# A new order list for attention and two feed-forward layers: the narrow token tile last, shared banks, interleaved pooled scores

## The chip, the cores and the metric

The kernel runs on one core of a Trainium2 chip. A core has five engines that work from instruction streams of their own: TensorE (PE in the profile, with its weight loads as PEld), VectorE (DVE), ScalarE (ACT), GpSimd (POOL) and SyncE (SP), which here only starts transfers. Sixteen DMA engines move data between HBM and the on-chip memory. Each engine takes its instructions strictly in program order, and waits at one until what it needs is there. The metric is the device time of one execution in microseconds, given as the median of several runs.

## What is computed

Attention over 4 batches, 8 heads and 576 positions, in two parts that are added: a pooled one (means over groups of 4 positions, so 144 by 144 scores, the result repeated 4 times) and a local one (only positions less than 4 apart). Its result is read as 2304 tokens of 512 values and goes through two feed-forward layers.

```python
def attention(q, k, v):                       # (4, 8, 576, 64)
    q_d, k_d, v_d = means over groups of 4    # (4, 8, 144, 64)
    out = repeat(softmax(q_d @ k_d.T / 8) @ v_d, 4)
    s = where(abs(i - j) < 4, q @ k.T / 8, -1e9)
    return out + softmax(s) @ v
x = attention(q, k, v) as (2304, 512)
h = x @ w_in                                  # 512 -> 2048
x2 = maximum(h, 0) ** 2 @ w_out               # 2048 -> 512
y = ((x2 @ w_a) * (x2 @ w_b)) @ w_out2        # 512 -> 1536 -> 512
```

## The kernel before

**Order.** The program is one hand-made list, `ORDER`, of tokens such as `H.0.3` or `ps.1.2.0.7`. A token calls one function, which writes its instructions; the order of the tokens is the order on every engine, and a letter (A, V, G, S) or a number in a token says which engine or which PSUM bank is used. So a token that stands earlier in the list puts its instructions ahead of all later ones on its engine, ready or not.

**First layer and attention.** Tokens are handled in units of 256, nine of them. `TILES` groups them to tiles: units 0-1, 2, 3-4, 5-6 and 7-8, that is 512, 256, 512, 512 and 512 tokens. For tile t, `H.t.f` computes block f of 16 of the hidden layer (12 matmuls, L648), `J` (three ScalarE steps, L655 to L658) and `L` (VectorE, L663) square it and split it into a high and a low part, and `P.t.f` (12 matmuls, L683) adds it to the four banks of x2. A matmul row in the profile is of 512 columns (a wide tile) or 256. The attention of units 0 to 4 (tokens b..) is done by TensorE in blocks with a band mask; that of units 5 to 8 (tokens l..) by VectorE and GpSimd, with products of 1792 columns (L416, L456) and sums (L424). The pooled attention (tokens p.., one per batch) computes scores in `scores` (L282): for each of 4 column groups ct of a batch and each of 2 heads, one call with two matmuls that use 64 of the 128 rows of the array, into one bank. Then come minima (L295), exponentials, transposes (L336) and values (L350). Attention of the units of one tile has to be complete before its `H`, and stands in the list between the blocks of the tile before.

**Warm-up.** `Z.k.n.bank` (L876) writes n transposes of the identity that nobody reads. There are 14 of them, 84 transposes, all ahead of `H.0.0`.

**Between the layers.** `E` copies a bank of x2 to the on-chip tile x2sb, `D` stores it in HBM (x2_d), and the second layer loads it from there. Of the last tile, only unit 7 goes this way; unit 8 stays on chip as xr2, split by `rh` (ScalarE) and `rl` (VectorE). `Q` frees the attention's buffers. `F.g.n` is step n of group g of what the second layer needs first: load and decode w_a and w_b (groups 0, 3, 4, 5) and load and split x2 of the first 1024 tokens, m = 0 (groups 1, 2, 6, 7). A split is a copy on ScalarE (L745, xb<-x2s), then a subtraction on VectorE (L742, xb<-x2s,xb).

**Second layer.** After the list, pool `ps` is closed and a pool of eight banks, `ps2`, is opened. The layer works in half sized blocks by a scheme with seven products: `hidden_span` computes for each j and m seven products for a and for b (12 wide matmuls in pairs, L916), and combines them in the banks and in the tiles r (r1 first: a ScalarE copy at L1012, which frees the bank for the next product). `hidden_rest` treats the unit left over from xr2 (48 narrow matmuls). Loads and splits for later steps, among them the second part m = 1 of x2, hang at numbered slots between the products (`put`).

Of the kernel before, what the change touches and what calls it, by code (L numbers as in the profile page):

```python
# [43 lines left out]
be.1.1 bc.1.0.0.V pj.0.0.2.V bm.0.1.0 bm.0.0.0 bx.0.0 bd.1.1 Z.11.6.7 pj.0.0.3.V pj.0.1.1.G sg be.0.0 pj.0.1.2.V
pq.0.A pj.0.1.3.V ps.0.2.0.4 ps.0.3.0.2 wd.1.S wd.8.S wc.1.A bd.0.0 wd.5.S ps.0.0.0.0 bq.0.1.S px.0.2.0 pe.0.2.0
wc.8.A bn.1.1.V wa.1 ps.0.0.1.4 wc.10.A ps.0.2.1.5 px.0.0.0 bn.0.0.V px.0.0.1 wa.8 bt.1.1.1.7 pe.0.0.1 pe.0.0.0 wh.8.G
px.0.2.1 px.0.3.0 pa.0.1.2 wd.0.S bc.1.1.1.V wa.10 wc.5.V pe.0.2.1 bt.0.0.0.6 wc.0.A wh.10.V Z.12.6.0 ps.0.1.0.1
wl.8.V pd.0.0 pd.0.2 wl.10.V bs.0.1.1.3 ps.0.3.1.0 bt.0.1.0.4 px.0.3.1 wa.5 bc.0.0.0.A pn.0.0.V pt.0.0.1.7 wh.1.A
# [87 lines left out]
def pooled_local_attention_two_ffn(  # L136
# [774 lines left out]
    def bank2():  # L911
        return ps2.tile([P, 512], F32, tag="b", name="bank")
# [408 lines left out]
```

## Time and profile before

| | before |
|---|---|
| median of 3 runs | 948.69 us (948.48 to 949.24) |
| the profiled execution | 950.97 us, of which the span is 949.2 us |
| mean granted clock of TensorE | 0.973 |
| busy: PE, DVE, ACT, POOL | 906.6, 568.2, 448.3, 302.5 us |
| first block of the first layer (`H.0.0`) starts | 65.8 us |
| last block of the first layer ends, second layer starts | 528 us |

The span is the time from the first to the last instruction on the core; 1.8 us of the execution lie around it. TensorE is busy nearly all the time, so the places to read are those where it is idle or where its granted clock is below 1. A timeline row gives the start, the time and the number of records of a run of like matmuls, and in brackets the idle time before it with the instruction that ended it.

### The profile page before, as it was taken

To read this page: it belongs to the slowest core of one execution; us is meant where nothing else is said; L and a number is where in the kernel's file an instruction comes from. 1 tells how busy PE (TensorE), PEld (TensorE's weight loads), DVE (VectorE), ACT (ScalarE), POOL (GpSimd) and SP (SyncE) were. 2 spreads that over 40 slices of the span, in tenths; PEclk is the share of its full clock that TensorE was granted. 3 is DMA by queue.
4 is the path that set the end of the run, shared out by engine and by line. 5 is a ranking of instruction groups with operands and counts; after the bars stand their busy time and mean duration, and the time that the engine had idled before them with its cause. 6 is when DMAs were issued, how large, how long until landed. Compare 5 with 4: busy or idle time off the path is not lost.

```text
span 949.2 us, 14089 instructions
## 1 busy us (share of the span) xinstructions
PE 906.6 (96%) x5084; PEld 755.9 (80%) x5084; DVE 568.2 (60%) x877; ACT 448.3 (47%) x1091; POOL 302.5 (32%) x286
## 2 busy tenths in 40 slices
PE   4799999999999999999999788999999999999998
PEld 3688877998877778887888576888888888788888
DVE  2768645442768768783114588686765654655451
ACT  3556456564534453334345445554454442554531
POOL 2232331211214541474011445565455450001010
PEclk9699999997999999999999798999999999999999
DMA  9575772641454204312300243875655649999522
GB/s 291 158 210 198 192 194 71 146 119 46 109 121 110 85 15 128 88 43 92 130 1 0 82 174 117 293 258 196 239 212 195 235 176 339 401 408 347 233 100 79
DMA packets 65854, 157.35 MB, mean 166 GB/s; under 512 B 7740, under 2 KB 11964, under 8 KB 65784
## 3 DMA queue, kind: packets, MB, share of 16 engines
q1 hardware_dynamic: 63336, 147.60, 45.2%
q0 software_dynamic: 2448, 8.85, 5.5%
q8 instruction: 40, 0.66, 0.3%
q14 instruction: 30, 0.25, 0.1%
HBM read 111.33 MB, written 45.09 MB: 165 GB/s over the span
## 4 chain that ended last, share of the span: by engine, by line
PE 90%; DVE 4%; ACT 1%; issue 1%; DVEq 0%
PE bank L916 40%; PE bank L648 21%; PE bank L683 21%; PE bank L282 2%; DVE xb L742 2%; PE bank L591 1%; PE bank L350 1%; PE bank L876 1%; PE bank L336 1%; PE bank L528 1%; PE bank L579 1%; DVE x2s L742 1%; DVE r L742 0%; PE bank L474 0%; DVE xx L496 0%
## 5 line engine op out<-in xcount | busy, mean ns | idle before, releaser
L916 PE MATMUL bank<-xb,wb 128*128 128x512 f32 x1008 | 236.6, 396 | 13.4 <-DVE xb L742 7.2
L916 PEld LDWEIGHTS bank<-xb,wb 128*128 128x128 f32 x1008 | 192.3, 192 | 55.7 <-DVE xb L742 9.0
L648 PE MATMUL bank<-xx,w 128*128 128x512 f32 (+1 forms) x960 | 214.8, 375 | 1.7 <-ACT xx L490 1.4
L683 PE MATMUL bank<-g,w 128*128 128x512 f32 (+1 forms) x960 | 212.3, 373 | 0.0
L648 PEld LDWEIGHTS bank<-xx,w 128*128 128x128 f32 x960 | 167.5, 190 | 36.9 <-ACT xx L490 3.3
L683 PEld LDWEIGHTS bank<-g,w 128*128 128x128 f32 x960 | 167.8, 190 | 32.9 <-issue 2.1
L916 PE MATMUL bank<-op,wo 128*128 128x512 f32 (+1 forms) x648 | 132.1, 366 | 1.6 <-DVE op L742 1.6
L916 PEld LDWEIGHTS bank<-op,wo 128*128 128x128 f32 x648 | 111.9, 189 | 21.9 <-DVE op L742 2.3
L663 DVE TENSOR_TENSOR g<-bank,g 128x512 fp32r<-128x512 f32 (+1 forms) x80 | 50.7, 634 | 119.1 <-ACT g L658 75.5
L742 POOL TENSOR_TENSOR wb<-raw,wb 128x256 fp32r<-128x256 f32 x96 | 80.8, 864 | 94.1 <-ACT wb L821 89.3
L655 ACT ACTIVATE bank<-bank 128x512 f32<-128x512 f32 (+1 forms) x80 | 43.3, 542 | 126.6 <-PE bank L648 126.6
L1012 ACT ACTIVATE r<-bank 128x512 f32<-128x512 f32 x72 | 42.8, 596 | 86.9 <-PE bank L916 80.3
L742 DVE TENSOR_TENSOR op<-ys,op 128x512 fp32r<-128x512 f32 x84 | 54.0, 707 | 31.3 <-ACT op L745 31.3
L966 DVE TENSOR_TENSOR r<-bank,r 128x512 f32<-128x512 f32 x48 | 32.9, 687 | 56.0 <-PE bank L916 41.7
L466 POOL TENSOR_TENSOR pv<-pv 128x768 f32<-128x768 f32 x16 | 34.9, 2181 | 84.2 <-DVE pv L456 84.2
L745 ACT ACTIVATE op<-ys 128x512 fp32r<-128x512 f32 x84 | 47.1, 624 | 25.1 <-PE bank L916 16.5
L222 DVE SCALAR_TENSOR_TENSOR raw<-raw,signs 128x512 uint32<-128x512 uint32 x68 | 49.0, 731 | 15.5 <-ACT signs L182 14.4
L658 ACT ACTIVATE g<-bank 128x512 fp32r<-128x512 f32 (+1 forms) x80 | 44.4, 555 | 20.9 <-PE bank L683 19.3
L742 POOL TENSOR_TENSOR wos<-raw,wos 128x256 fp32r<-128x256 f32 x48 | 43.1, 913 | 34.0 <-ACT wos L821 30.1
L821 ACT ACTIVATE wb<-raw 128x256 fp32r<-128x256 f32 x96 | 37.5, 425 | 16.4 <-DVE raw L222 8.8
L656 ACT ACTIVATE bank<-bank 128x512 f32<-128x512 f32 (+1 forms) x80 | 43.1, 539 | 2.5
L813 DVE TENSOR_TENSOR raw<-raw 128x256 f32<-128x256 f32 x72 | 41.9, 607 | 0.8
(121 smaller groups left out, 1021.9 us busy)
## 6 DMA issues: line engine op xcount, KB each, us to landing
ys<-y_d SPq DMA_DIRECT2D x42, 512.0 KB, 7.9
y_d<-r SPq DMA_DIRECT2D x72, 256.0 KB, 2.2
wo_d<-wos SPq DMA_DIRECT2D x48, 256.0 KB, 2.8
raw<-in_w_out SPq DMA_DIRECT2D x16, 511.8 KB, 3.9
raw<-in_w_in SPq DMA_DIRECT2D x16, 511.8 KB, 4.4
wo<-wo_d SPq DMA_DIRECT2D x24, 256.0 KB, 6.9
wo<-wo_d SPq DMA_DIRECT2D x12, 512.0 KB, 7.0
raw<-in_w_b SPq DMA_DIRECT2D x12, 511.8 KB, 4.1
```

The costliest lines, as they stand in the source:

```text
L222: nc.vector.scalar_tensor_tensor(out=self.v, in0=self.v, scalar=13, in1=self.signs, op0=ALU.logical_shift_right, op1=ALU.bitwise_or,)
L648: nc.tensor.matmul(out=h, lhsT=wi[f].w[:, a, ct * P:(ct + 1) * P], rhs=xT[t, ct][:, b], start=(n == 0), stop=(n == 3 * NCT - 1),)
L655: nc.scalar.activation(out=h, in_=h, func=AF.Relu)
L656: nc.scalar.activation(out=h, in_=h, func=AF.Square)
L658: nc.scalar.activation(out=self.g[0], in_=h, func=AF.Copy)
L663: nc.vector.tensor_tensor(out=self.g[1], in0=h, in1=self.g[0].bitcast(F32), op=ALU.subtract)
L683: nc.tensor.matmul(out=x2[t][et], lhsT=wo[f].w[:, a, et * P:(et + 1) * P], rhs=g[b], start=(f == 0 and (a, b) == (0, 0)), stop=(f == F1 - ...
L742: engine.tensor_tensor(out=out, in0=in0, in1=in1, op=ALU.subtract)
L745: nc.scalar.activation(out=tile_hi, in_=src, func=AF.Copy)
L813: nc.vector.tensor_tensor(out=self.of(key), in0=self.of(a), in1=self.of(b), op=op)
L916: nc.tensor.matmul(out=out, lhsT=blk[:, a, cols:cols + P], rhs=rhs[b], start=(start and n == 0), stop=(stop and n == 2), skip_group_check= ...
L1012: nc.scalar.activation(out=r[n][:, w], in_=bk["X", w], func=AF.Copy)
```

## The change

- `TILES` becomes units 0-1, 2-3, 4-5, 6-7 and 8: the tile of 256 tokens comes last instead of second. All of it stays on chip as xr2, so that `evict` and `store` no longer treat a half.
- `scores` is called as often as before, but the first head's call only takes its bank; the second head's call writes the four matmuls of both heads, one head after the other in turn, into two banks.
- The second layer takes its banks from the first layer's pool, in the turn 6, 7, 0, 1, 2, 3, 4, 5, instead of from a new pool.
- The loads and splits of x2 for m = 1 (24 steps) move from slots of the second layer into the list, as groups 8 to 11 of `F`.
- `ORDER` is written anew: other places, other engines for copies and splits. Of `Z` 8 tokens with 32 transposes are left, 6 of them ahead of `H.0.0`.
- Buffers: xl gets a place that is freed by the new token `R`, wr has 23 in place of 24 tiles, gq 4 in place of 3. Three loads in the second layer's output part are split or moved by a slot.

```diff
-TILES = ((0, 2), (2, 1), (3, 2), (5, 2), (7, 2))
+TILES = ((0, 2), (2, 2), (4, 2), (6, 2), (8, 1))
...
 ORDER = """
...
-P.4.15 F.6.6 F.7.5 F.7.6 F.6.7 F.3.6 F.6.8 F.6.9 F.7.7 F.7.8 F.7.9 F.3.7 F.5.5 F.3.8 F.5.6 rh.3 rl.3 E.4.0.V E.4.3.V
-F.5.7 F.7.10 F.5.8 rh.0 F.5.9 rh.1 F.3.9 F.6.10 rl.1 F.5.10 rh.2 rl.2 rl.0 E.4.2.V E.4.1.A F.3.10 D.4.0
...
+F.6.9 J.4.15 L.4.15 P.4.15 F.5.2 F.6.10 F.11.1 F.5.3 F.5.4 F.5.5 F.5.6 rh.2 rh.1 F.7.10 F.5.7 F.5.8 F.10.1 F.10.2
+F.10.3 F.10.4 F.11.2 F.5.9 rh.3 rl.3 F.10.5 F.11.3 F.11.4 F.10.6 F.11.5 rl.2 F.11.6 F.10.7 F.5.10 F.10.8 rh.0 F.11.7
+rl.0 rl.1 F.10.9 F.10.10 F.11.8 F.11.9 F.11.10
...
         def scores(self, ct, h2, kind):
-            lo = 64 * h2
-            s = bank(kind)
+            self.s[ct, h2] = bank(kind)[:KC, :2 * SG].rearrange("p (c k) -> p c k", c=2)
+            if h2 == 0:
+                return
             for qc in range(2):
-                nc.tensor.matmul(
-                    out=s[:KC, qc * SG:(qc + 1) * SG],
-                    lhsT=self.qd[lo:lo + 64, ct * SG + qc * KC:ct * SG + (qc + 1) * KC],
-                    rhs=self.kd[lo:lo + 64, ct * SG:(ct + 1) * SG],
-                    start=True, stop=True,
-                )
-            self.s[ct, h2] = s[:KC, :2 * SG].rearrange("p (c k) -> p c k", c=2)
+                for h in range(2):
+                    lo = 64 * h
+                    nc.tensor.matmul(
+                        out=self.s[ct, h][:, qc],
+                        lhsT=self.qd[lo:lo + 64, ct * SG + qc * KC:ct * SG + (qc + 1) * KC],
+                        rhs=self.kd[lo:lo + 64, ct * SG:(ct + 1) * SG],
+                        start=True, stop=True,
+                    )
...
+    early += [units[1, 0][:1], units[1, 1][:1], units[1, 0][1:], units[1, 1][1:]]
...
-        gq = ctx.enter_context(tc.tile_pool(name="gq", bufs=3))
-        wr = ctx.enter_context(tc.tile_pool(name="wr", bufs=24))
+        wr = ctx.enter_context(tc.tile_pool(name="wr", bufs=23))
+
+    def last_tile():
+        nonlocal gq
+        xs.close()
+        gq = ctx.enter_context(tc.tile_pool(name="gq", bufs=4))
...
-    pp.close()
-    ps2 = ctx.enter_context(tc.tile_pool(name="ps2", bufs=8, space=PSUM, reuse_waits="tile"))
+    banks2 = cycle((6, 7, 0, 1, 2, 3, 4, 5))
...
     def bank2():
-        return ps2.tile([P, 512], F32, tag="b", name="bank")
+        return bank(next(banks2))
...
-    put(0, units[1, 0][:1])
-    put(0, units[1, 1][:1])
-    put(9, [fn for pair in zip(units[1, 0][1:], units[1, 1][1:]) for fn in pair], 2)
```

**On TensorE ahead of `H.0.0`.** L528 and L579 (L530 and L581 after) are scores and transposes of the band attention, L876 (L872) the warm-up, L282 (L287) pooled scores. Before:

```order
L876 MATMUL bank_272<-ident_102 128x128 x6
L282 MATMUL bank_295<-qkd_152 72x144 x2
L282 MATMUL bank_298<-qkd_152 72x144 x2
L282 MATMUL bank_310<-qkd_152 72x144 x2
L282 MATMUL bank_326<-qkd_152 72x144 x2
L282 MATMUL bank_330<-qkd_152 72x144 x2
L579 MATMUL bank_339<-ident_102,blk_197 70x128 x4
L579 MATMUL bank_364<-ident_102,blk_264 70x128 x4
L876 MATMUL bank_372<-ident_102 128x128 x6
L282 MATMUL bank_379<-qkd_152 72x144 x2
```

And after the change:

```order
L872 MATMUL bank_268<-ident_102 128x128 x4
L530 MATMUL bank_290<-kb_147,qb_145 64x70 x8
L287 MATMUL bank_289<-qkd_122 72x144
L287 MATMUL bank_299<-qkd_122 72x144
L287 MATMUL bank_289<-qkd_122 72x144
L287 MATMUL bank_299<-qkd_122 72x144
L287 MATMUL bank_217<-qkd_122 72x144
L287 MATMUL bank_308<-qkd_122 72x144
L287 MATMUL bank_217<-qkd_122 72x144
L287 MATMUL bank_308<-qkd_122 72x144
```

The two matmuls of a call stood together on one bank; now each alternates with one of the other head on another bank. Between here and `H.0.0` ten more warm-up tokens followed before; one follows now.

**On VectorE in the third wide tile,** between the squares (L663, L665) of two blocks of the first layer. L416, L424 and L456 (L418, L426 and L458 after) are the products and sums of the local attention. Before:

```order
L663 TENSOR_TENSOR g_3313<-bank_3250,g_3268 128x512
L186 TENSOR_SCALAR o_sb_103<-bank_3285 128x144
L416 TENSOR_TENSOR p_3340<-qt_3309,kt_3310 128x1792
L456 TENSOR_TENSOR pv_3366<-vt_3355,sc_2814 128x1792
L424 TENSOR_REDUCE sc_3017<-p_3216 128x4x7
```

And after the change:

```order
L452 TENSOR_TENSOR sc_2795<-sc_2795,m2_3087 128x112
L418 TENSOR_TENSOR p_3096<-qt_3083,kt_3084 128x1792
L458 TENSOR_TENSOR pv_3098<-vt_2799,sc_2795 128x1792
L426 TENSOR_REDUCE sc_3100<-p_3096 128x4x7
L418 TENSOR_TENSOR p_3102<-qt_3027,kt_3028 128x1792
L665 TENSOR_TENSOR g_3106<-bank_3014,g_3094 128x512
L665 TENSOR_TENSOR g_3133<-bank_3034,g_3131 128x512
```

Four long rows in place of two or three stand in one piece ahead of a square, and two squares then stand together.

**On ScalarE where the second layer starts.** The first r row is the copy that frees the first product's bank. Before:

```order
L745 ACTIVATE xb_4989<-x2s_4367 128x512
L821 ACTIVATE wb_4993<-raw_4527 128x256
L720 ACTIVATE xr2_4965<-bank_4395 128x256
L182 ACTIVATE x2sb_4968<-bank_4394 128x256
L821 ACTIVATE wb_5001<-raw_4646 128x256
L1012 ACTIVATE r_5040<-bank_5033 128x512
L1012 ACTIVATE r_5040<-bank_5042 128x512
```

And after the change:

```order
L711 ACTIVATE xr2_4941<-bank_4407 128x256
L736 ACTIVATE xb_4992<-x2s_4836 128x512
L736 ACTIVATE xb_4995<-x2s_4838 128x512
L736 ACTIVATE xb_4998<-x2s_4685 128x512
L736 ACTIVATE xb_5001<-x2s_4689 128x512
L736 ACTIVATE xb_5004<-x2s_4691 128x512
L1004 ACTIVATE r_5022<-bank_5015 128x512
L1004 ACTIVATE r_5022<-bank_5024 128x512
```

The copies of m = 1 (x2s_4685 to 4691 and 4832 to 4838) now stand ahead of the first r; before, they came after the fourth.

## Rows read from the trace of the kernel before

**Rows 1.** The page's part 1: busy time of each engine, share of span, instructions.
```profile
PE 906.6 (96%) x5084; PEld 755.9 (80%) x5084; DVE 568.2 (60%) x877; ACT 448.3 (47%) x1091; POOL 302.5 (32%) x286
```

**Rows 2.** TensorE's waits: what for, us in total, times, longest.
```profile
PE bank L528 <- DMA kb<-in_k_t: 10.1, 3, 4.8
PE bank L916 <- DVE xb L742: 7.2, 2, 3.8
...
PE bank L591 <- ACT a L324: 2.4, 1, 2.4
```

**Rows 3.** Stretches: length, then busy PE, PEld, DVE, ACT, POOL; clock, DMA share, GB/s.
```profile
0.00:27.70 27.70, 11.43 (x122) 9.70 (x122) 9.59 (x21) 10.73 (x52) 5.35 (x10) 0.88 0.92 293
...
40.80:52.00 11.20, 11.13 (x90) 9.76 (x90) 5.66 (x16) 6.16 (x30) 2.51 (x4) 0.54 0.96 249
52.00:65.80 13.80, 13.80 (x245) 12.58 (x243) 10.15 (x23) 6.15 (x17) 6.09 (x5) 1.00 0.68 203
...
216.00:226.00 10.00, 9.90 (x69) 9.20 (x70) 0.73 (x3) 2.68 (x10) 0.88 (x2) 0.50 0.23 41
...
248.00:351.00 103.00, 102.10 (x501) 80.16 (x500) 79.00 (x91) 44.70 (x115) 42.76 (x31) 1.00 0.40 96
...
528.40:598.00 69.60, 56.24 (x264) 46.27 (x264) 53.96 (x77) 34.05 (x73) 34.51 (x34) 0.88 0.43 151
...
598.00:949.20 351.20, 345.65 (x1682) 292.38 (x1680) 207.68 (x320) 158.88 (x322) 109.70 (x120) 1.00 0.67 246
```

**Rows 4.** Groups of TensorE by line in 40.8 to 65.8 us: records, busy, mean ns.
```profile
L876 PE MATMUL bank<-ident 128*128 128x128 f32 x60 | 10.7, 336 | 0.0
```

**Rows 5.** The same from 0 to 65.8 us, pooled scores.
```profile
L282 PE MATMUL bank<-qkd 64*72 64x144 f32 x32 | 7.5, 414 | 3.3 <-ACT qkd L182 3.3
```

**Rows 6.** The same over the whole span.
```profile
L282 PE MATMUL bank<-qkd 64*72 64x144 f32 x128 | 22.2, 331 | 3.6 <-ACT qkd L182 3.3 <-ACT aT L182 0.2
```

**Rows 7.** TensorE's timeline around 210 to 233 us: start, time, operation, records.
```profile
210.76 0.71 PE L282 MATMUL bank<-qkd 64*72 64x144 f32 x4
211.40 1.70 PE L683 MATMUL bank<-g,w 128*128 128x256 f32 x12
...
216.10 1.97 PE L591 MATMUL bank<-blk,vb 70*64 70x64 f32 x32 [2.37 <-ACT a L324]
218.01 2.93 PE L683 MATMUL bank<-g,w 128*128 128x256 f32 x12
...
227.31 1.60 PE L683 MATMUL bank<-g,w 128*128 128x256 f32 x12
...
232.04 0.72 PE L282 MATMUL bank<-qkd 64*72 64x144 f32 x8
```

**Rows 8.** TensorE's timeline where the second layer starts.
```profile
528.21 2.88 PE L916 MATMUL bank<-xb,wb 128*128 128x512 f32 x12
537.27 19.47 PE L916 MATMUL bank<-xb,wb 128*128 128x512 f32 x72 [6.17 <-DVE x2sb L184]
556.57 5.92 PE L916 MATMUL bank<-xr,wb 128*128 128x256 f32 x48
...
569.28 4.33 PE L916 MATMUL bank<-xb,wb 128*128 128x512 f32 x12 [3.82 <-DVE xb L742]
576.97 15.47 PE L916 MATMUL bank<-xb,wb 128*128 128x512 f32 x59 [3.36 <-DVE xb L742]
...
598.03 38.27 PE L916 MATMUL bank<-xb,wb 128*128 128x512 f32 x168
```

**Rows 9.** Groups of VectorE by line and shape: records, busy, mean ns.
```profile
L813 DVE TENSOR_TENSOR raw<-raw 128x256 f32<-128x256 f32 x72 | 41.9, 607 | 0.8
L416 DVE TENSOR_TENSOR p<-qt,kt 128x1792 f32<-128x1792 f32 x16 | 34.7, 2167 | 0.0
...
L742 DVE TENSOR_TENSOR xb<-x2s,xb 128x512 fp32r<-128x512 f32 x28 | 25.0, 922 | 2.1 <-ACT xb L745 2.1
...
L742 DVE TENSOR_TENSOR x2s<-x2s 128x512 f32<-128x512 f32 x8 | 7.0, 890 | 0.0
```

More of the change, by code (lines that the diff above doesn't have):

```diff
@@ L1 @@
+from itertools import cycle
 from contextlib import ExitStack
@@ L44 @@
[L44 to L48, printed above, removed]
@@ L164, in pooled_local_attention_two_ffn @@
     gp = ctx.enter_context(tc.tile_pool(name="gp", bufs=4))
-    pp = ctx.enter_context(ExitStack())
-    ps = pp.enter_context(tc.tile_pool(name="ps", bufs=1, space=PSUM))
+    ps = ctx.enter_context(tc.tile_pool(name="ps", bufs=1, space=PSUM))
+    xs = ctx.enter_context(ExitStack())
+    xl = xs.enter_context(tc.tile_pool(name="xl", bufs=2, side="right"))
     lp = ctx.enter_context(ExitStack())
@@ L199, in pooled_local_attention_two_ffn, with new_signs @@
     signs = []
-    def new_signs(pool, tag):
-        words = pool.tile([P, 2, 512], U32, tag=tag, name="signs")
+    def new_signs(pool, tag, n=2):
+        words = pool.tile([P, n, 512], U32, tag=tag, name="signs")
         nc.gpsimd.memset(words, 0)
-        signs[:] = [words[:, 0], words[:, 1]]
+        signs[:] = [words[:, k] for k in range(n)]
     class Weight:
@@ L692, in evict @@
         width = TILES[t][1] * T1
-        if t == LAST:
-            width -= T1
-            key = t, 0
-        else:
-            key = t, e2
+        key = t, e2
         if key not in x2sb:
             x2sb[key] = st.tile([P, 1024], F32, tag="stage", name="x2sb")
-        o = x2sb[key][:, (et if t == LAST else c) * width:][:, :width]
-        copy(engine, o, x2[t][et][:, :width])
+        copy(engine, x2sb[key][:, c * width:(c + 1) * width], x2[t][et])
     def store(t, e2):
         i, count = TILES[t]
-        if t == LAST:
-            count -= 1
-            src, ets = x2sb[t, 0], slice(0, NCT)
-        else:
-            src, ets = x2sb[t, e2], slice(2 * e2, 2 * e2 + 2)
         width = count * T1
-        n = ets.stop - ets.start
         nc.sync.dma_start(
-            out=x2_d[:, ets, i * T1:i * T1 + width],
-            in_=src[:, :n * width].rearrange("p (e t) -> p e t", e=n),
+            out=x2_d[:, 2 * e2:2 * e2 + 2, i * T1:i * T1 + width],
+            in_=x2sb[t, e2][:, :2 * width].rearrange("p (e t) -> p e t", e=2),
         )
@@ L724, in rest_low @@
         nc.vector.tensor_tensor(
-            out=x[:, 1, et % 2], in0=x2[LAST][et][:, -T1:], in1=x[:, 0, et % 2].bitcast(F32),
+            out=x[:, 1, et % 2], in0=x2[LAST][et], in1=x[:, 0, et % 2].bitcast(F32),
             op=ALU.subtract,
@@ L1208, in pooled_local_attention_two_ffn @@
     base = SLOTS * (NP - 1)
-    put(base + 11, [lambda: load_wo("A11", range(NP)), lambda: load_wo("A22", (0, 1))])
-    put(base + 20, [lambda: load_next(8)])
+    put(base + 11, [lambda: load_wo("A11", range(NP)), lambda: load_wo("A22", (0,))])
+    put(base + 20, [lambda: load_wo("A22", (1,)), lambda: load_next(8)])
     put(base + 17, [lambda: load_wo2("S3", (0, 2, 4))])
```

170 lines of the change are left out of this document (87 added, 83 removed).

## The prediction

> **What bounds the kernel now.** TensorE. The page's first part has it busy for 96% of the span [rows 1]; the other engines matter only where they make it wait, or where it waits so long that its clock falls to the lower of two levels (1.2 in place of 2.4 GHz, a granted clock of 0.50). So I read the list of TensorE's waits first [rows 2], then a table of stretches with the granted clock [rows 3], then the timeline in the stretches that are not full. There are three.
>
> The start: `H.0.0` comes at 65.8 us. Until 27.7 us the DMA engines are 0.92 busy and TensorE waits for inputs; from 40.8 us on it is busy without a gap, at clock 0.54 up to 52 us and 1.00 from there [rows 3], and 10.7 us of these 25 are warm-up transposes [rows 4]. The first tile boundary: a wait of 2.37 us, then 10 us at clock 0.50 [rows 3, 7]. The start of the second layer: from 528.4 to 598 us TensorE is busy 56.2 of 69.6 us at 0.88 [rows 3], with waits of 6.17, 3.82 and 3.36 us [rows 2, 8].
>
> **The change part by part.** The sum is made against the profiled execution, 950.97 us.
>
> *Start.* Ahead of `H.0.0`, 24 transposes are left of 84. At 336 ns [rows 4] the 60 removed are worth 20 us if each were on the path, but only the 10.7 us in 40.8 to 65.8 us stand where TensorE never idles; the others fill waits for data. Counting what the program orders put ahead of `H.0.0` and pricing each instruction by its mean in the trace, TensorE's work falls from 33.0 to 23.4 us, VectorE's from 40.8 to 36.1, ScalarE's from 39.8 to 34.3, GpSimd's rises from 20.2 to 23.0, and the bytes to be loaded fall from 13.85 to 11.22 MB, 9 us less at the 293 GB/s of the first row of [rows 3]. VectorE gives the smallest gain of these, 4.7 us, TensorE the largest, 9.6. I take −7. Bounds: −12 (warm-up and bytes both on the path) and +2 (`H.0.0` where it was, and 2 us more at clock 0.50, since less runs ahead of it; in [rows 3] the low clock lasted 11 us beside other work).
>
> The clock fell or stayed low here in spite of transposes: in 40.8 to 52 us TensorE was 11.13 of 11.2 us busy, at 0.54 [rows 3]. The Trainium skill ("TensorE: Matmul & The Clock Gate", Part 4: PE-mode transpose) says that a transpose does not count as busy time for the clock in the way a matmul does. By that rule taking the warm-up away costs nothing in clock, and the start is worth the −9.6 of TensorE's load; without it, what stands in the bound of +2. The trace agrees for 40.8 to 52 us but doesn't settle it, as 1.00 is reached at 52 us with transposes among other work.
>
> *Pooled scores.* All 32 calls take 22.2 us [rows 6], 7.5 of them ahead of `H.0.0` [rows 5] and counted above; 14.7 us for 24 calls remain. A call that stands alone takes 0.71 us and the next matmul starts 0.64 us behind its start, at 210.76 and 211.40 [rows 7]; where the calls of both heads happened to stand together, eight records took 0.72 us at 232.04 [rows 7]: the two row halves run side by side. The change puts the heads together in all 12 remaining groups, 12 x 0.72 = 8.6 us, so −6.1. Bounds −7 and 0.
>
> *First boundary.* The wait at 216.10 us and the low clock behind it cost 2.4 us and half of 9 us, 6.9 together [rows 3, 7]: 12 narrow matmuls took 2.93 us there and 1.60 at 227.31. The narrow tile, in which this falls, has gone to the end, so −6.9.
>
> What comes in its place: tile 0 now must cover block 3 (unit 3) besides block 2, within the same 110 us of TensorE. In the order of the changed program the last chain ahead of `H.1.0` (exponentials of block 3 behind `J.0.15` on ScalarE, then totals, transposes, copies, values, outputs, split) stands behind TensorE's last work of tile 0. Some eight short steps of 0.4 to 0.7 us, less what TensorE still has, leave 2 to 3 us, and the low clock after it as much again, as the wait of 2.37 us did [rows 7]: +5, from 0 to +8.
>
> *Later boundaries.* At tile 1 to 2, two steps of unit 6, each some 2.1 us as L416 [rows 9], stand on VectorE ahead of the sum that ends unit 5: +3 (0 to +5). In tile 2, VectorE now has units 6 and 7 to do: by counts 88 us of work in some 95 us of TensorE's, where the fullest stretch of before had 79.0 in 103 [rows 3]. The order shows four long steps in one piece ahead of a square; products and sums with their small steps make some 11 us in which TensorE has about 9 us in hand, and the same again ahead of tile 3: +5 (0 to +10).
>
> *Start of the second layer.* Between 528.4 and 598 us stand 168 wide matmuls and 96 narrow ones. 168 wide ones took 38.3 us at 598.03, 228 ns each, and 48 narrow ones 5.8 at 556.57 [rows 8], so 49.8 us of the 69.6 are work and some 20 are lost. In the changed order two waits go: the banks no longer wait for the whole first layer (6.17 us, a copy of x2 for the store), and the splits of m = 1, behind which VectorE was late at 569 and 577 us [rows 8], are in the list. But the latter now stand ahead of the first r copy on ScalarE, and the last of these waits for VectorE. Behind the last square VectorE has, up to the subtraction that it needs: five steps of decoding at some 0.61, nine splits of 0.92, four subtractions of 0.89 and two small ones, 15.8 us [rows 9]. The square, the fourth of four steps of some 0.4 us, ends 1.6 us after the last hidden block, so r comes at about 18.6 us. TensorE has after that block 4.3 us of projections and 24 wide matmuls, 5.4 us, 9.8 in all. It waits about 9 us, and loses 3 at the low clock as it did from 537.27 on (72 matmuls in 19.47 us in place of 16.4 [rows 8]), 13 in all with 1 for what is small. Against 20 that is −6.5 (rounded). With splits at two thirds of the mean the work is 10.8 us and the loss 7: −13. With all steps at a third over the mean the wait is 14 us, the loss 17, and with one more wait as at 569.28 [rows 8] and its slow clock 23: +3.
>
> *Nothing or little.* Two warm-up tokens within tile 0 and 1: +1. Simpler stores, buffers, slots of the output part: 0, since TensorE was 345.7 of the 351 us busy behind 598 us [rows 3] and no matmul is added there; ±2.
>
> *Sum:* −7 −6.1 −6.9 +5 +3 +5 −6.5 +1 = −11.5 us, 939.5 us as a profiled run. The median of the runs stands 2.3 us below the profiled one, so the forecast is **937 us**.
>
> **The rivals.**
>
> *A, slower: a backlog in the fixed order of VectorE and ScalarE.* It is one thing at three places: the splits ahead of r, the local steps ahead of the sums of units 5 and 6, and the chain of block 3. For it: VectorE is fuller than before in tiles 1 and 2, and it has one queue. Against: before, it stood 60% busy and let TensorE through with 9 us between two squares. It decides from 11.5 us more of stalls than I have reckoned: all at their upper bounds give 3 + 2 + 5 + 9.5 = 19.5 more, and 15 of these **952 us**.
>
> *B, the scores don't overlap* as the one place at 232.04 lets me think, since now the two heads change at each matmul and not after two. Then 6.1 us stay, and 2 at the start: **945 us**.
>
> *C, the start does not move:* the inputs or VectorE set it, and tile 0 begins at the low clock. Then +2 in place of −7: **946 us**. By the rule on transposes above the clock has no part in it.
>
> *D, the second layer starts without a wait,* VectorE at its faster pace and the boundaries of the tiles covered: −6.5 and −8 more: **923 us**.
>
> **How the numbers follow.** Forecast 0.46, A 0.18, B 0.12, C 0.12, D 0.12. The forecast's own range is 930 to 943. The range that should hold it 8 times in 10 reaches from D to near A: 922 to 952. A measurement of this kernel can tell some 0.2%, 1.9 us, from no change. Faster: forecast, B, C and D but for what of B and C ends near 947, 0.76; same 0.07; slower, most of A, 0.17.
>
> **What would show it.** Steps right: `H.0.0` at 57 to 60 us; the score records in sets of eight in 0.72 us; no stretch at clock 0.50 near 216 us, but one of a few us where tile 1 starts; one wait of 5 to 12 us in TensorE's list at the third product of the second layer, on ScalarE's r copy, and no others there. Wrong: `H.0.0` still at 65 us (C), single score calls of 1.3 us a pair (B), waits of the squares or of tile 2 and 3 above 5 us each (A), none at the r copy (D).

## The result and the profile after the change

The changed kernel takes **936.0 us**, median of 4 runs (931.9 to 936.5), beside 949.0 for the kernel before (4 runs): a ratio of 0.984, with an interval of 0.981 to 0.987. The forecast was 937 in a range of 922 to 952.

The profiled execution of after is the shortest of these four, 931.85 us with a span of 929.3; the other three lie 4 to 5 us above it (two further ones on record took 931.1 and 934.8). One of the experiments below, `e6_scores_block`, executes the same instructions with the four matmuls of a score call in another order, and its profile has a span of 934.2. There the first projections (L685) start at 64.58 us in place of 61.72 and the second layer at 517.6 in place of 512.85: the difference lies ahead of the second layer, more than half of it at the start. The longer executions of after may differ from its profile in the same way; they have no trace, so this is not shown.

From the page of after, and then TensorE's waits as in [rows 2] (total, times, longest):

```profile
PE 890.7 (96%) x5032; PEld 739.8 (80%) x5032; DVE 567.4 (61%) x864; ACT 451.2 (49%) x1098; POOL 299.6 (32%) x288
```

```profile
PE bank L911 <- ACT r L1004: 11.8, 1, 11.8
PE bank L530 <- DMA kb<-in_k_t: 6.9, 2, 5.5
PE bank L581 <- DVE blk L572: 3.5, 2, 2.6
PE bank L650 <- DVE g L665: 2.3, 2, 1.9
PE bank L476 <- POOL x L470: 1.7, 2, 0.9
```

One wait of 11.8 us stands at the top, the one forecast at 9: the third product of the second layer waits for ScalarE's `r`. The other waits are short or lie in the start.

The timeline of TensorE in after where the first layer starts (start, duration, then line, operation and count), and a row of the stretches (busy time of PE, PEld, DVE, ACT, POOL; granted clock, DMA share, GB/s):

```profile
53.95 4.30 PE L650 MATMUL bank<-xx,w 128*128 128x512 f32 x12
...
58.82 3.06 PE L650 MATMUL bank<-xx,w 128*128 128x512 f32 x12
61.72 2.89 PE L685 MATMUL bank<-g,w 128*128 128x512 f32 x12
```

```profile
40.00:53.95 13.95, 13.95 (x154) 11.53 (x152) 10.01 (x22) 6.53 (x25) 7.63 (x8) 0.50 1.02 297
```

`H.0.0` has come forward from 65.78 to 53.95 us, and TensorE is full ahead of it, at half its clock: the first 12 wide matmuls still take 4.30 us, the next 3.06.

The second layer's start, TensorE and then ScalarE (what stands in brackets is the idle time before the row and what ended it):

```profile
508.53 4.48 PE L685 MATMUL bank<-g,w 128*128 128x256 f32 x36
512.85 5.63 PE L911 MATMUL bank<-xb,wb 128*128 128x512 f32 x24
530.32 15.88 PE L911 MATMUL bank<-xb,wb 128*128 128x512 f32 x60 [11.85 <-ACT r L1004]
...
576.61 23.76 PE L911 MATMUL bank<-xb,wb 128*128 128x512 f32 x104
```

```profile
517.98 0.63 ACT L736 ACTIVATE xb<-x2s 128x512 fp32r<-128x512 f32 x1
521.59 0.63 ACT L736 ACTIVATE xb<-x2s 128x512 fp32r<-128x512 f32 x1 [2.98 <-POOL x2s L733]
523.95 0.63 ACT L736 ACTIVATE xb<-x2s 128x512 fp32r<-128x512 f32 x1 [1.74 <-POOL x2s L733]
...
527.60 2.19 ACT L736 ACTIVATE xb<-x2s 128x512 fp32r<-128x512 f32 x4 [0.75 <-DVE x2s L733]
529.70 1.06 ACT L1004 ACTIVATE r<-bank 128x512 f32<-128x512 f32 x2
```

The first product is done at about 515.7 us, but the copy that frees its bank starts at 529.70. In between ScalarE has splits for m = 1 in its queue and waits three times for the subtractions that these need. TensorE stands from 518.5 to 530.3 us. Still, the 168 wide and 96 narrow matmuls [rows 8] now take 63.8 us (512.85 to 576.61) and took 69.8 (528.21 to 598.03).

By stretches, profile against profile (spans 949.2 and 929.3):

| stretch | before | after | difference | forecast |
|---|---|---|---|---|
| up to `H.0.0` | 65.8 | 53.9 | −11.8 | −7 |
| first layer behind it | 462.4 | 458.9 | −3.5 | +1.0 |
| first 168 + 96 matmuls of the second layer | 69.8 | 63.8 | −6.1 | −6.5 |
| rest | 351.2 | 352.7 | +1.5 | 0 |
| sum | 949.2 | 929.3 | −19.9 | −12.5 |

The medians differ by 13.0 us only, since the profiled execution of before lay 2.0 above its median and that of after 4.2 below.

### The profile page after: what moved, and what is told of

It reads as the page before. It is cut to its first block, busy times and chain, and to the rows that moved or that the text cites. A ratio compares the mean times of both kernels' runs of the same rounds, so it can differ in the third digit from the quotient of the medians.

```text
span 929.3 us, 13981 instructions
## 1 busy us (share of the span) xinstructions
PE 890.7 (96%) x5032; PEld 739.8 (80%) x5032; DVE 567.4 (61%) x864; ACT 451.2 (49%) x1098; POOL 299.6 (32%) x288
## 4 chain that ended last, share of the span: by engine, by line
PE 85%; DMA 4%; DVE 3%; ACT 3%; POOL 3%; issue 1%; SPq 0%; DVEq 0%; POOLq 0%; ACTq 0%
PE bank L911 40%; PE bank L650 20%; PE bank L685 19%; PE bank L593 2%; PE bank L352 1%; PE bank L338 1%; PE bank L581 1%; DMA qkd<-in_qk_p 1%; DMA wo<-wo_d 1%; DMA ys<-y_d 1%; PE bank L530 1%; DMA kt<-in_k_l 1%; POOL pv L468 1%; DMA vd<-in_v_p 1%; POOL pv L469 1%
## 5 line engine op out<-in xcount | busy, mean ns | idle before, releaser
L911 PE MATMUL bank<-xb,wb 128*128 128x512 f32 x1008 | 232.1, 392 | 11.8 <-ACT r L1004 11.8
L911 PEld LDWEIGHTS bank<-xb,wb 128*128 128x128 f32 x1008 | 190.1, 189 | 51.6 <-ACT r L1004 12.3
L685 PE MATMUL bank<-g,w 128*128 128x512 f32 (+1 forms) x960 | 210.3, 371 | 0.0
L685 PEld LDWEIGHTS bank<-g,w 128*128 128x128 f32 x960 | 166.3, 189 | 31.4 <-issue 0.8
L665 DVE TENSOR_TENSOR g<-bank,g 128x512 fp32r<-128x512 f32 (+1 forms) x80 | 50.6, 634 | 108.9 <-PE bank L685 70.7
L733 POOL TENSOR_TENSOR wb<-raw,wb 128x256 fp32r<-128x256 f32 x96 | 77.9, 832 | 80.1 <-ACT wb L812 75.1
L468 POOL TENSOR_TENSOR pv<-pv 128x768 f32<-128x768 f32 x16 | 32.8, 2053 | 68.5 <-DVE pv L458 68.5
L184 ACT ACTIVATE signs<-raw 128x512 f16<-128x512 bf16 x57 | 43.1, 783 | 1.0 <-DMA raw<-in_w_a 0.9
```

Of the source, the lines that this page charges most:

```text
L184: engine.activation(out=out, in_=in_, func=AF.Copy, scale=scale)
L665: nc.vector.tensor_tensor(out=self.g[1], in0=h, in1=self.g[0].bitcast(F32), op=ALU.subtract)
L685: nc.tensor.matmul(out=x2[t][et], lhsT=wo[f].w[:, a, et * P:(et + 1) * P], rhs=g[b], start=(f == 0 and (a, b) == (0, 0)), stop=(f == F1 - ...
L733: engine.tensor_tensor(out=out, in0=in0, in1=in1, op=ALU.subtract)
L911: nc.tensor.matmul(out=out, lhsT=blk[:, a, cols:cols + P], rhs=rhs[b], start=(start and n == 0), stop=(stop and n == 2), skip_group_check= ...
```

## The experiments

They ask four things: what holds the `r` copy (e1, e12, e5), why the score calls are faster (e2, e6), what sets the start (e3, e7 to e11), and how near VectorE is to the bound in the first layer (e4, e9). Unless said otherwise the edit is made in the kernel after, and a ratio is against the kernel before, run on the same chip.

### What holds the second layer's start

**e1_r_first** takes the steps of groups 10 and 11 behind their loads and the last one of group 5 from the end of the list and puts them in slots of the second layer, where they are issued behind the first `r` copies:

```diff
-F.6.9 J.4.15 L.4.15 P.4.15 F.5.2 F.6.10 F.11.1 F.5.3 F.5.4 F.5.5 F.5.6 rh.2 rh.1 F.7.10 F.5.7 F.5.8 F.10.1 F.10.2
...
+F.6.9 J.4.15 L.4.15 P.4.15 F.5.2 F.6.10 F.5.3 F.5.4 F.5.5 F.5.6 rh.2 rh.1 F.7.10 F.5.7 F.5.8 F.5.9 rh.3 rl.3 rl.2 rh.0
...
+    put(4, [lambda g=g, n=n: early[g][n]() for g, n in (
...
```

> The changed kernel with the 20 last steps of m = 1 (groups 10 and 11) and the last block of w_b taken out of the list and hung at the second layer's slots from 4 on, two at a slot, so that the first r copies stand ahead of them on ScalarE. Theory (queue): TensorE waits 11.85 us at the third product of the second layer because r stands behind these splits. Then this wait falls to 0 to 4 us, the low clock behind it goes, and the whole takes 924 to 929 us. Rival (buffers or x2 itself): the third product would wait for its own split operand or the weights anyway; the wait stays above 8 us and the time at 934 to 937. Second rival: VectorE is as late with the splits of m = 1 as it was before the change, waits of some 7 us come back at the first product of m = 1, and the time is 931 to 936.

Measured: **924.4 us** (922.2 to 926.8), ratio 0.977 (0.973 to 0.981). ScalarE's `r` row and TensorE's timeline in e1:

```profile
517.09 1.09 ACT L1006 ACTIVATE r<-bank 128x512 f32<-128x512 f32 x2
```

```profile
512.58 16.51 PE L910 MATMUL bank<-xb,wb 128*128 128x512 f32 x72
529.25 3.46 PE L910 MATMUL bank<-xb,wb 128*128 128x512 f32 x12 [0.16 <-DVE r L960]
...
542.52 19.35 PE L910 MATMUL bank<-xb,wb 128*128 128x512 f32 x78 [2.67 <-DVE r L966]
...
567.46 2.91 PE L910 MATMUL bank<-xb,wb 128*128 128x512 f32 x12
```

`r` is copied at 517.09 in place of 529.70, 72 matmuls run in one piece at full pace, and the stretch takes 54.9 us (512.58 to 567.46) in place of 63.8. The second layer began at about the same time as in after (512.85), so 8.9 of the 9.2 us between the spans (920.1 and 929.3) are made here. The work moved costs one wait of 2.67 us later. The copy was held by the queue in front of it, not by the product or by the banks.

**e12_r_first_b** does the same, but leaves `F.5.10` in the list and gives the buffers their old counts:

```diff
-        wr = ctx.enter_context(tc.tile_pool(name="wr", bufs=23))
+        wr = ctx.enter_context(tc.tile_pool(name="wr", bufs=24))
...
-        gq = ctx.enter_context(tc.tile_pool(name="gq", bufs=4))
+        gq = ctx.enter_context(tc.tile_pool(name="gq", bufs=3))
```

> The changed kernel with the 20 last steps of m = 1 at the second layer's slots from 4 on, as in the first experiment, but with the last block of w_b left in the list and the buffers of before (24 weight tiles and 3 of the others). Theory (queue): again no wait above 4 us at the third product, and 922 to 927 us. Rival (the moved block of w_b or the buffers made the gain of the first experiment): a wait above 6 us there and 930 to 937 us.

Measured: 926.4 us (923.4 to 927.7), ratio 0.978 (0.975 to 0.981). The two rows that answer to e1's:

```profile
514.94 16.51 PE L910 MATMUL bank<-xb,wb 128*128 128x512 f32 x72
...
545.51 17.98 PE L910 MATMUL bank<-xb,wb 128*128 128x512 f32 x78 [2.79 <-DVE r L966]
```

The same stretch without the long wait, 54.1 us to 569.07, and no measurable difference from e1. The step and the buffers do not matter; the queue does.

**e5_own_banks** gives the second layer a pool of its own again, as before:

```diff
...
-    banks2 = cycle((6, 7, 0, 1, 2, 3, 4, 5))
+    pp.close()
+    ps2 = ctx.enter_context(tc.tile_pool(name="ps2", bufs=8, space=PSUM, reuse_waits="tile"))
...
```

> The changed kernel with the second layer's banks from a new pool again, as before the change. Theory (banks gate the start): the third bank in turn is one of the last tile's x2 banks, which VectorE reads last at some 529 us behind the splits; TensorE waits there after one product in place of two, and 5 us of work that stood ahead of the wait come behind it: waits of 13 to 15 us in all, and 939 to 942 us. Rival (the r copy alone sets it): the wait stays at 11 to 12 us at the third product and the time within 1.5 us of the changed kernel.

Measured: 935.2 us (930.8 to 936.1), ratio 0.984 (0.982 to 0.987), as after. TensorE in e5:

```profile
511.97 2.91 PE L913 MATMUL bank<-xb,wb 128*128 128x512 f32 x12
528.26 19.02 PE L913 MATMUL bank<-xb,wb 128*128 128x512 f32 x72 [13.38 <-DVE xr L716]
```

The wait comes one product earlier and on VectorE's `xr`, as the prediction has it for a pool that waits for the whole first layer, but the stretch is only 2.0 us longer (511.97 to 577.70), and the rest of the second layer 1.4 shorter (351.3 against 352.7). The wait for `r` lies behind the one that the shared pool removes and ends at about the same time. And the 1.4 us in the rest belong to the pool: the ten profiles with the shared pool have 352.6 to 353.2 us there, the four with a pool of its own (before, e5, e8, e11) 351.1 to 351.3. With the shared pool TensorE waits once more near the end, in after here:

```profile
908.24 16.95 PE L911 MATMUL bank<-op,wo 128*128 128x256 f32 x138 [0.98 <-ACT ro L1139]
```

So by the profiles the shared pool gives 2.0 us at the second layer's start and costs 1.4 behind it, and the times can't tell it from nothing.

### Why the score calls are faster

**e2_scores_apart** puts the old `scores` back, two matmuls at each head's own call:

```diff
-            self.s[ct, h2] = bank(kind)[:KC, :2 * SG].rearrange("p (c k) -> p c k", c=2)
-            if h2 == 0:
-                return
+            lo = 64 * h2
+            s = bank(kind)
...
```

> The changed kernel with the old scores function: two matmuls of one head at that head's own call, at the places of the new list. Theory (side by side only when the heads alternate or adjoin): calls that stand apart take 0.64 us each again; pooled scores take 11.7 us in all in the changed kernel and would take 14 to 18 us, the whole 938 to 943 us. Rival (the gain is in the list, whose calls mostly adjoin): the scores stay under 13 us and the whole within 1.5 us of the changed kernel.

In the list of after, the first head's call of seven of the 16 groups stands ahead of the step that scales the pooled queries; in e2 these scores are computed from unfinished inputs. Measured: 946.9 us (941.9 to 947.8), ratio 0.998 (0.996 to 1.001). **e6_scores_block** keeps the four matmuls in one call, head by head:

```diff
-            for qc in range(2):
-                for h in range(2):
+            for h in range(2):
+                for qc in range(2):
```

> The changed kernel with the four score matmuls of a group written head by head (both of head 0, then both of head 1) in place of in turn, at the same place. Theory (adjoining calls are enough): the two row halves run side by side all the same, a group of eight records takes 0.72 us, the scores 11.5 to 13 us in all, and the whole stays within 1.5 us of the changed kernel. Rival (only the turn by turn order runs side by side): a group takes 1.3 us, the scores 20 to 23 us, the whole 5 to 9 us slower.

Measured: 935.0 us (932.4 to 935.9), ratio 0.985 (0.982 to 0.987). The groups of all 128 score records in after, e2 and e6, in this order (busy time, mean ns, idle before):

```profile
L287 PE MATMUL bank<-qkd 64*72 64x144 f32 x128 | 11.7, 304 | 0.2
```

```profile
L284 PE MATMUL bank<-qkd 64*72 64x144 f32 x128 | 22.9, 335 | 7.2 <-POOL qkd L188 4.1 <-DVE qkd L275 1.3 <-ACT qkd L184 0.8
```

```profile
L287 PE MATMUL bank<-qkd 64*72 64x144 f32 x128 | 13.0, 325 | 0.0
```

Apart, the records take 22.9 us (22.2 in before, [rows 6]); together 11.7 or 13.0. Most of the 1.3 us between the last two lies in the 32 records ahead of `H.0.0` (2.9 us in after, 3.9 in e6); behind it the other 96 take 8.8 us in after, 9.0 in e6 and 13.6 in e2. So it is enough that the calls of both heads adjoin. Taking the heads in turn adds nothing that the time shows. e2 is 10.8 us above after by the medians, but this is no clean measure of the edit: its calls come too early in the list, and 7.2 us of waits for `qkd` are of its own making. The records' times are.

### What sets the start

The first projections are the mark for the start here. In after and the four experiments that change nothing ahead of `H.0.0` (e1, e4, e5, e12) they start at 61.72, 61.29, 61.67, 60.83 and 64.13 us, so a difference of some 3 us between two profiles says nothing by itself.

**e3_warm_later** adds one warm-up token of 18 transposes ahead of the step `bw.0.0.7`:

```diff
-bt.1.0.0.0 pt.0.0.1.6 bt.1.1.0.3 bw.0.0.7 pt.0.1.0.1
+bt.1.0.0.0 pt.0.0.1.6 bt.1.1.0.3 Z.8.18.5 bw.0.0.7 pt.0.1.0.1
...
```

> The changed kernel with 18 more warm-up transposes ahead of the first band value matmuls, at about 37.6 us. In the changed kernel the granted clock is 0.50 from 30 to 57 us though TensorE is busy without a gap from 36 us on; before the change it came back at 52 us behind 18 transposes. Theory (transposes bring the clock back): the clock is 1.00 from some 42 us on, the 4 us of transposes are paid back, the first block of the first layer starts at 50 to 54 us and its 12 matmuls take 2.7 in place of 4.3 us; the whole is 0 to 5 us faster. Rival (transposes do not count for the clock): the clock stays at 0.50 until the wide matmuls, and the whole is 3 to 9 us slower.

Measured: 936.8 us (936.1 to 937.3), ratio 0.990 (0.986 to 0.993). TensorE in e3, then two stretches of e3:

```profile
41.56 2.42 PE L872 MATMUL bank<-ident 128*128 128x128 f32 x18
43.92 1.15 PE L593 MATMUL bank<-aTb,vb 70*64 70x64 f32 x32
...
54.44 1.20 PE L650 MATMUL bank<-xx,w 128*128 128x512 f32 x4 [1.11 <-ACT o_sb L184]
58.28 3.70 PE L650 MATMUL bank<-xx,w 128*128 128x512 f32 x8 [2.65 <-DVE xx L186]
```

```profile
40.00:42.00 2.00, 2.00 (x14) 1.86 (x12) 1.68 (x5) 0.59 (x1) 0.44 (x1) 0.50 0.85 288
42.00:44.00 2.00, 2.00 (x19) 1.83 (x20) 1.97 (x6) 0.83 (x5) 0.00 (x0) 0.96 1.06 329
```

The clock comes up from 0.50 to 0.96 while TensorE does nothing but transposes, as it has since 38.92 us (those of the attention, then the 18), and 32 value matmuls take 1.15 us behind it (1.98 in after, at 0.50). The rule of the Trainium skill weighed ahead of the result ("TensorE: Matmul & The Clock Gate", Part 4: PE-mode transpose), that a transpose doesn't count as busy for the clock in the way a matmul does, doesn't agree with these rows. But that it takes the 18 added ones is not shown. In e6, which has none of them, the clock is at 1.00 from 42 to 44 us too, and the value matmuls there are as fast:

```profile
42.50 1.15 PE L593 MATMUL bank<-aTb,vb 70*64 70x64 f32 x32
```

The start gains nothing by the faster clock: TensorE now waits 1.11 us for ScalarE and 2.65 for VectorE (1.23 and 2.64 in e6), and the first projections come at 65.77 us in e3 and 64.58 in e6, later than in after, whose clock stays at 0.50 until about 57 us.

**e7_no_warm** takes away all warm-up ahead of `H.0.0`; no other step is touched:

```diff
-bq.0.0.S Z.3.4.7 pl.0 pg.0.0.0.S pa.0.1.0 Z.6.4.5 bs.0.1.0.6 bm.0.1.0 bv.0.0.S bq.1.0.S bs.0.0.0.5 bq.0.1.S sg Z.1.4.0
...
```

> The changed kernel without the 24 warm-up transposes ahead of the first block of the first layer; the two later tokens stay. Theory (VectorE sets the start): the wide matmuls begin within 1.5 us of 54 us, at a low clock for some more us, and the whole is within 2 us of the changed kernel. Rival (TensorE sets the start): the first block comes 4 to 6 us earlier, and the whole is 3 to 6 us faster. Second rival (the clock sets it): TensorE stays at 0.50 throughout, the first block comes 2 to 5 us later and the whole is 2 to 8 us slower.

Measured: 933.6 us (932.5 to 936.3), ratio 0.984 (0.982 to 0.986), as after. The first 12 wide matmuls start at 56.03 us and take 5.53 (3.06 for the next 12), and the first projections come at 65.03 (64.58 in e6). The 24 transposes left in after buy nothing that the time shows.

**e8_before_less_warm** is the kernel *before* with 2 in place of 6 transposes at each token, 28 in place of 84:

```diff
-Z.6.6.7 Z.4.6.4 bh.1.3.V bs.2.1.0.7 wh.5.A bh.1.2.A
+Z.6.2.7 Z.4.2.4 bh.1.3.V bs.2.1.0.7 wh.5.A bh.1.2.A
...
```

> The kernel before with 2 transposes in each of its 14 warm-up tokens in place of 6, so 28 in place of 84, and nothing else. Theory (the transposes stood on the path of the start): the first block of the first layer comes 5 to 9 us earlier, at 57 to 61 us, and the whole is 4 to 9 us faster. Rival (VectorE or the inputs set the start before the change as well): the first block stays at 64 to 67 us and the whole within 1.5 us. Second rival (clock): without them the clock stays at 0.50 up to the first wide matmuls, and the whole is 2 to 6 us slower.

Measured: 945.0 us (944.3 to 946.5), ratio 0.995 (0.993 to 0.997). TensorE in e8, then two stretches:

```profile
66.65 1.19 PE L648 MATMUL bank<-xx,w 128*128 128x512 f32 x4
```

```profile
40.00:60.00 20.00, 18.69 (x160) 15.32 (x161) 13.00 (x27) 9.22 (x39) 8.78 (x9) 0.50 0.78 214
213.00:227.00 14.00, 14.00 (x142) 12.63 (x140) 6.01 (x18) 9.01 (x38) 2.87 (x3) 1.00 0.40 76
```

`H.0.0` is 0.9 us *later* than in before (66.65, 65.78): with 56 transposes fewer the clock stays at 0.50, and the same other work fills TensorE for 18.69 of 20 us. The gain lies elsewhere: around 216 us, where before waited 2.37 us and then ran slowly [rows 3, 7], TensorE is full at 1.00. From the last score call ahead of that place to the band transposes behind it, the same instructions in both, e8 takes 11.7 us (214.79 to 226.51) and before 18.5 (213.03 to 231.51), 6.8 less. Nothing was edited there: the shifts from the start decide whether TensorE waits.

**e11_before_warm_block**, *before* again, puts 18 transposes at one place in place of the ten later tokens of 6:

```diff
-Z.2.6.5 pe.0.3.1 bc.0.1.0.A bm.0.1.1 ps.0.1.1.3
+Z.2.18.5 pe.0.3.1 bc.0.1.0.A bm.0.1.1 ps.0.1.1.3
...
```

> The kernel before with the four warm-up tokens up to 37 us as they are, and the other ten, 60 transposes from 41 us on, replaced by one block of 18 at the place of the first of them. Theory (TensorE set the start before the change, and its transposes were more than the clock needs): the clock is 1.00 from some 44 us on, the first block of the first layer comes at 57 to 62 us in place of 65.8, and the whole is 3 to 8 us faster. Rival (VectorE and the inputs set it): waits for them appear on TensorE, the first block stays at 64 to 67 us, and the whole is faster only by what the wait at the first tile boundary, gone with 28 transposes in place of 84, gives: 0 to 5 us.

Measured: 948.8 us (946.5 to 950.0), ratio 1.001 (0.999 to 1.002). TensorE in e11:

```profile
51.71 1.23 PE L350 MATMUL bank<-aT,vd 72*64 72x144 f32 x8 [2.49 <-ACT a L309]
66.97 1.20 PE L648 MATMUL bank<-xx,w 128*128 128x512 f32 x4
```

Where transposes are missing, a wait of 2.49 us for the exponentials `a` of ScalarE stands in their place, and `H.0.0` comes at 66.97. So the warm-up of before didn't set its start: it filled time in which TensorE would have waited or run slowly. The wait near 216 us is gone here as in e8, and the whole is no shorter all the same: the first projections come at 79.36 us, 4.2 later than in before (75.15; 76.91 in e8).

**e10_weights_later** is e1 with the decoding and the splits of weights 8 and 15 moved from ahead of `H.0.0` to behind it and `H.0.1`:

```diff
-ps.0.0.1.2 bn.0.1.V pe.0.1.1 pa.0.1.2 pd.0.1 wc.8.V px.0.0.1 px.0.0.0 be.1.0 Z.0.4.1 pn.0.1.G bs.1.0.1.7 wa.8 wh.8.V
+ps.0.0.1.2 bn.0.1.V pe.0.1.1 pa.0.1.2 pd.0.1 px.0.0.1 px.0.0.0 be.1.0 Z.0.4.1 pn.0.1.G bs.1.0.1.7 bt.0.0.1.6
...
+bl.1.3.V H.0.0 wc.8.V wa.8 wh.8.V wl.8.G wa.6 bs.2.0.0.6 bq.2.1.S wd.17.S bv.2.1.S wh.5.G
...
```

> The kernel of the first experiment (r copies first) with the decoding and splitting of two first-layer weight blocks, the third of w_out and the ninth of w_in, moved from ahead of the first hidden block to just behind the first two, so 3.3 us less on VectorE, 0.9 us less on GpSimd ahead of it. Theory (VectorE sets the start): the first projections come 1.5 to 3.5 us earlier than in the first experiment, and the whole takes 921 to 923 us in place of 924.4. Rival (the inputs or TensorE set it): the start does not move, and the whole is 924 to 927 us. Second rival: the two blocks, or the later loads that wait for their buffers, come too late within the first tile, and TensorE waits there; 925 to 932 us.

Measured: 931.5 us (929.5 to 932.8), ratio 0.983 (0.979 to 0.987), some 7 us worse than e1. TensorE in e10:

```profile
52.39 1.98 PE L592 MATMUL bank<-aTb,vb 70*64 70x64 f32 x32 [2.12 <-DMA vb<-in_v_t]
...
70.02 0.73 PE L649 MATMUL bank<-xx,w 128*128 128x512 f32 x2 [1.43 <-DVE w L185]
71.73 6.93 PE L649 MATMUL bank<-xx,w 128*128 128x512 f32 x22 [0.97 <-DVE w L234]
```

A wait for an input appears ahead of `H.0.0`, and two waits for weights behind it. The edit was meant to relieve VectorE and ScalarE and made the loads late, so it doesn't tell what those engines cost.

### How near VectorE is to the bound

**e9_minima_thrice** computes the row minima of band units 0 and 1 three times, 5.9 us more on VectorE ahead of `H.0.0`:

```diff
-            nc.vector.tensor_reduce(out=mx, in_=p, axis=AX.X, op=ALU.min)
+            for _ in range(3 if self.i < 2 else 1):
+                nc.vector.tensor_reduce(out=mx, in_=p, axis=AX.X, op=ALU.min)
```

> The changed kernel with the minima of the band scores of units 0 and 1 computed three times over on VectorE, eight more steps of 0.73 us, 5.9 us in all, ahead of the first block of the first layer. Theory (VectorE sets the start): the first projections, at 61.7 to 64.6 us in the changed kernel, come 3 to 6 us later, and the whole is 3 to 6 us slower than its 936. Rival (TensorE at its low clock, or the inputs, set it): less than 1.5 us later, and the whole within 2 us.

Measured: 937.8 us (936.1 to 938.1), ratio 0.990 (0.985 to 0.994). The first projections start at 67.63 us, 3.5 to 6.8 later than in the five profiles that share after's start, yet the whole is 1.7 longer by the medians, within the intervals. VectorE has a part in the start, but the whole doesn't pay for it one for one.

**e4_products_twice** does the products of three of the four heads of local unit 6 twice, 6.5 us more on VectorE in the third tile:

```diff
-            nc.vector.tensor_tensor(
...
+            for _ in range(2 if self.i == 6 and h else 1):
+                nc.vector.tensor_tensor(
...
```

> The changed kernel with three of the long products of unit 6 done twice on VectorE in the third tile, 6.5 us more work. Theory (VectorE is nearly the bound in that tile): the tile gets 3 to 6.5 us longer and the waits of TensorE for squares there, 2.3 us now, grow by that; the whole 939 to 943 us. Rival (TensorE has work in hand between the squares): the whole stays within 1.5 us of the changed kernel.

Measured: 940.6 us (938.1 to 941.7), ratio 0.992 (0.989 to 0.995), 4.6 us above after. TensorE's wait for the squares in e4:

```profile
PE bank L651 <- DVE g L666: 3.9, 2, 3.4
```

It was 2.3 in after. Part of the cost shows there. The medians put 4.6 of 6.5 us on the path; the two profiles, whose starts agree (first projections at 61.67 and 61.72 us), put all of it there, as the second layer begins 7.1 us later (519.92 and 512.85). So VectorE is the bound in that tile, or nearly.

## Why the prediction was right, and where only its sum was

**The sum.** Its terms, −7 −6.1 −6.9 +5 +3 +5 −6.5 +1, add up to −12.5; the text has −11.5, a slip of 1 us. By its own terms it should have said 938.5 us as a profiled run and 936.2 as a median. The medians did fall by 13.0, but the profiles by 19.9, and single terms were further off than either: errors of both signs cancelled. So that the total came out is luck in good part.

**Right: the score calls.** Forecast −6.1 behind `H.0.0`, measured −5.9: 96 records take 8.8 us there and took 14.7. A call in after, and behind it the next matmul at 146.54 us:

```profile
145.90 0.71 PE L287 MATMUL bank<-qkd 64*72 64x144 f32 x8
```

Rival B is out. The place at 232.04 us, where the heads adjoin without taking turns, could not tell whether taking turns would spoil the gain; e6 and after show that the order within the four doesn't matter.

**Right: the first boundary.** No wait and no low clock stand near 216 us. e8 bears out the price, as the same place is 6.8 us shorter there without the wait. It also shows that before could have had this with fewer transposes.

**Right in mechanism: the second layer's start.** The wait stands where it was forecast, for the reason given; e1 and e12 show it by removing the queue. Its size was 11.85 in place of 9 us, since `r` came 21.2 us behind the start of the last projections and not 18.6 behind the last hidden block, while TensorE reached it as reckoned, 10.0 us behind against 9.8. The stretch came out at −6.1 against −6.5, so what lay beyond the wait was priced somewhat too high. The sum for `r` had steps of VectorE alone; of ScalarE's three waits in the rows above, the two longest (2.98 and 1.74 us) are for subtractions of GpSimd. The share given to the shared pool (6.17 us of [rows 2] gone) was not a gain of its own (e5).

**Wrong in size: the start.** −7 forecast; −11.8 in the profile, some −9 in the executions that make the median, by e6's first projections. The failed step is the one that took TensorE's load with its warm-up and VectorE's load as the two ends. e8 and e11 show that the transposes of before didn't set its start, e7 that those of after don't either. Two chains run nearly side by side there: with the clock low TensorE is full (after), with the clock up it waits for VectorE and ScalarE (e3). What shortened both by 9 to 12 us is not shown. Along the traces after is 4.1 us ahead of before at the first pooled scores (23.63 and 27.75 us), 6.1 at the first transposes of `a` (34.80 and 40.87) and 11.8 at `H.0.0`, so half of it is there before the stretch in which TensorE is full. The busy time up to `H.0.0` fell by 8.1 us on TensorE, 2.4 on VectorE and 4.0 on ScalarE (reckoned: 9.6, 4.7 and 5.5). The 9 us of fewer bytes fit in size, but the DMA engines moved 14.6 MB up to there in before and 13.7 in after, only 0.9 less, loads for later among them; and e10, which touched the weights, made other loads late. This stays open. Nor are 60 transposes worth 20 us: the 336 ns of [rows 4] is the length of one record beside others that overlap it, and the 60 records took 10.7 us together.

**Wrong in size: the boundaries of tiles 1, 2 and 3.** +13 forecast. The waits there in after are 0.25, then 0.77 and 0.90 for GpSimd's `x`, then 0.38 and 1.94 for the squares, 4.2 us together, and the clock is 1.00 at all of them:

```profile
162.18 1.15 PE L593 MATMUL bank<-blk,vb 70*64 70x64 f32 x32 [0.25 <-ACT xx L184]
...
276.06 0.66 PE L476 MATMUL bank<-ident,x 128*128 128x128 f32 x4 [0.90 <-POOL x L470]
...
310.42 1.88 PE L650 MATMUL bank<-xx,w 128*128 128x512 f32 x7 [1.94 <-DVE g L665]
```

The two waits for `x`, 1.7 us, stand where +3 was forecast. Of the other +10, two steps failed. At tile 1 the chain of block 3 was counted with 2 to 3 us beyond TensorE's work and a low clock behind it; TensorE still had the last projections of tile 0 (3.03 us from 163.26) and small steps of other tokens, and waited 0.25 us. In tile 2 the long VectorE steps were counted as stalls, 11 us less a guessed 9 in hand; ahead of the longest wait TensorE had 11.8 us in hand (296.66 to 308.48). The four long steps took 8.1, and it was a wait of VectorE itself, for a sum of GpSimd, that made the square late:

```profile
307.73 2.03 DVE L418 TENSOR_TENSOR p<-qt,kt 128x1792 f32<-128x1792 f32 x1 [2.30 <-POOL x L470]
309.68 1.28 DVE L665 TENSOR_TENSOR g<-bank,g 128x512 fp32r<-128x512 f32 x2
```

VectorE itself was nearly as full as reckoned (88 of 95 us), as e4 and the row of the third tile say (41.19 of 46.5 us busy):

```profile
263.50:310.00 46.50, 43.66 (x220) 34.68 (x220) 41.19 (x45) 22.06 (x55) 19.24 (x14) 1.00 0.46 107
```

Rival A is out, though by e4 further work for VectorE in this tile would be paid for at once. So are C, as the start did move, and D, as the second layer did wait.

**Not foreseen.** Behind `H.0.0`, the wide matmuls of the first layer's hidden blocks take 3.2 us more (190.5, 187.3), 1.1 of it in the first twelve, at the low clock (4.30, 3.16); and 48 more band scores stand there (192 records in 8.5 us, 144 in 6.2), 2.3 us that had been ahead of the start. So part of the start's −11.8 is work put off. The rest of the second layer is 1.5 us longer, within the ±2 given; by e5 this is the price of the shared pool, to which the prediction gave none.

## What to carry to other kernels

Read the queue of the engine that frees the bank which the next product needs: work for later, put in ahead of that copy, held up TensorE for 11.85 us here. Moving it behind gained 9.2 us of the span (e1, 924.4 us, faster than both kernels). The small matmuls that use different halves of the rows gained as soon as they stood next to each other, in either order. Where several chains end at nearly the same time, as at this start, neither taking work from one engine (e7) nor a faster clock (e3, e6) brought the end forward: add work to each in turn and see which one answers before putting a price on it.

## What the runs showed of the hardware beyond this

- The clock rose with nothing but transposes on TensorE: in e3, where it stood still for 3.51 us and then did only these from 38.92 to 43.92 us, from 0.50 (40 to 42 us) to 0.96 (42 to 44). In e8, with 56 fewer than before, it read 0.50 from 40 to 60 us, and in before it was back at 52.
- The granted clock of a row isn't always the clock of the work: in e7 it is 1.00 from 50 to 56 us, while 32 value matmuls take 1.98 us at 51.46, as at 0.50 in after, and 12 wide matmuls right behind 5.53 us, against 3.06 for the next 12.

```profile
50.00:56.00 6.00, 6.00 (x84) 5.32 (x80) 5.18 (x11) 2.98 (x9) 4.37 (x6) 1.00 1.02 302
```

```profile
56.03 5.53 PE L649 MATMUL bank<-xx,w 128*128 128x512 f32 x12
62.13 3.06 PE L649 MATMUL bank<-xx,w 128*128 128x512 f32 x12
```

- At the second layer's start four split subtractions of VectorE took 5.12 us in after (from 515.31), 1.28 each, where the 28 of this kind take 0.87 on average and the forecast had 0.92. GpSimd was at work beside them all the time (513.63 to 521.56 us), in part on two subtractions of the same size that took 3.38. From 504 to 511 us, while GpSimd stood still, the steps of this kind took 0.65 to 0.69 us. That the two slow each other fits this, but was not tried, and one step of e1 (at 520.76 us) took 0.69 inside a row of GpSimd (518.17 to 524.31).
